# A fused attention and expert kernel: attention rows stored as float32, half pairs made for the first eight tiles only

## The chip, the cores and the metric

The kernel runs on one core of one Trainium2 chip. The metric is the device time of one execution in microseconds: the median of three runs is 897.36 us, from 895.99 to 898.08. The core's engines run side by side, each with a queue of its own: TensorE (PE in the profile, its weight loads PEld), VectorE (DVE), ScalarE (ACT), GpSimd (POOL) and SyncE (SP), which here only issues DMAs. ScalarE and GpSimd issue DMAs too.

## The reference

Three steps follow each other on 2304 tokens of 512 values. The first is an attention through 32 memory slots a head, for 4 batches and 8 heads:

```python
a = softmax(phi, axis=2)                       # over the 32 slots
k_m = einsum('bhsm,bhsd->bhmd', a, k); v_m = einsum('bhsm,bhsd->bhmd', a, v)
x = softmax(q @ k_m.T / 8) @ v_m               # as rows of 512 values, one a token
logits = x @ w_gate + log1p(exp(x @ w_noise)) * noise
out[mask] += weight * (relu(x[mask] @ w1[e]) @ w2[e])     # the two best of 8 experts
h = out @ w_in; result = (h * cos(h)) @ w_out
```

The second routes each token to its two best experts of 8 (512 to 1024 to 512), the third is a dense block (512 to 2048 to 512). All is float32; the kernel makes its products from pairs of halves: a float16 high part, and a float16 low part that is the float32 value less the high part.

## The kernel before

**Attention.** The 2304 tokens are 18 tiles of 128 rows. `k_gen` (L629) makes the 32 keys and values of a batch, `t_gen` (L728) one tile: scores, softmax, transposes, then the product `x` in PSUM. ScalarE copies `x` to `xs`, 128 x 512 in float32 (L769), and 32 gate columns to the routing's buffer (L775). Then the rows are split: ScalarE copies `xs` to float16 (L780), GpSimd subtracts that from `xs` for the low half (L782), and SP stores both, `hl`, as one row of 1024 float16 values in the DRAM tensor `xd` (L783). For the last two tiles this step is held back behind the routing's logarithm and the first gathers (L779, L781, L838 to L840). `xs` and `hl` take their slots from the pool `lp`, which has seven of 2 KB a partition (L77); later the experts' outputs, a zero tile and a scratch tile of ScalarE's share it.

**Routing.** `route` (L413) runs twice on VectorE, for tiles 0 to 7 and for tiles 8 to 17. Each run ends with a table of indices: `idxA` (L510), from tiles 0 to 7 alone, two columns of 128 slots for each expert (the first group); and `idxB` (L513), three columns for each expert, the last one 96 wide (the second group, 352 slots), of any tile. The one-hot rows for the table are made at L496 and L501.

**Experts.** `gather_x` (L906) has GpSimd gather 128 rows of `xd` into a tile `xg` (three buffers) by an indirect DMA, and SP turn it with a transposing DMA into `xT`, halves and all. `turn_x` (L920) is the turn by itself, for the groups that are gathered long ahead. `l1` (L924) multiplies a group by w1 in TensorE, `l1_out` (L942) makes the halves of the result on ScalarE and VectorE; `l2` (L950) multiplies 128 rows by w2. The weights come as float32 and are split by ScalarE (`w_hi`) and VectorE (`w_lo`). The first expert is special: its first group starts once `idxA` is there, while the second routing runs; `l2_first` (L972) then does its w2 products, high halves of w2 first and low halves behind, while the second group is gathered.

**Order.** What the engines run in which order is written out by hand: `at(t, f, ...)` (L86) plans a call at a time, with a lead that sets its priority, and `issue` sorts the calls. `gated(key)` and `chain(key, ...)` (L282, L286) put an instruction behind a named one on its own engine. The change moves calls between L835 and L856 and between L1262 and L1318. `tA` (L841) is the planned time of the step between the two routings, and `x` in L1292 to L1318 the running time of the experts. `overflow` (L1001) is a loop for experts with more than 608 rows.

Of the kernel before, what the change touches and what calls it, by code (L numbers as in the profile page):

```python
# [21 lines left out]
P = 128  # L22
# [43 lines left out]
def fused_kernel(ctx, tc, phiT, qT, kv, wgn, noise, w1, w2, wi, wo, out):  # L66
    nc = tc.nc
    V, A, G, T, SP = nc.vector, nc.scalar, nc.gpsimd, nc.tensor, nc.sync

    xd = nc.dram_tensor("xd", (N, 2 * DM), F16).ap()  # L70
    yd = nc.dram_tensor("yd", (YROWS, DM), F32).ap()
    wst = nc.dram_tensor("wst", (2 * NCH, P, 2048), F16).ap()

# [97 lines left out]
    def l2k(shape, dt, name):  # L171
        return lp.tile(shape, dt, tag="l", name=name)
# [555 lines left out]
    def t_gen(t):  # L728

        sc = scb[:, t % 2]  # L730
        for p0, n, b in segs(t):
            c0 = (t % 8) * P + p0
            for c in range(4):
                T.matmul(sc[p0:p0 + n, 64 * c:64 * c + 64], lhsT=qt[t // 8][:, c, c0:c0 + n],  # L734
                         rhs=bdkt[b][:, c, :], start=True, stop=True)
        yield
        sv = sc.rearrange("p (h m) -> p h m", m=M)
        mx = ap.tile([P, H], F32, tag="smx", name="smx")
        V.tensor_reduce(mx, sv, axis=AX.X, op=OP.max)
        dk = sds[t % 4]  # L740
        dv = dk[:, :, 0:M]
        V.tensor_tensor(dv, sv, mx[:, :, None].to_broadcast([P, H, M]), op=OP.subtract)
        yield
        A.activation(dv, dv, AF.Exp, scale=0.125)
        yield
        su = ap.tile([P, H], F32, tag="ssm", name="ssm")
        V.tensor_reduce(su, dk, axis=AX.X, op=OP.add)
        last[f"t{t}V"] = V.reciprocal(su, su)
        d = ap.tile([P, 2 * P], F32, tag="d", name="d")
        G.tensor_tensor(d.rearrange("p (h m) -> p h m", m=M), dv, su[:, :, None].to_broadcast([P, H, M]), op=OP.mult)  # L750
        yield
        pt = ptb[:, t % 2]
        for g in range(2):
            last[f"t{t}T"] = T.transpose(pt[:, g * P:(g + 1) * P], d[:, g * P:(g + 1) * P], ident)
        eT = ap.tile([P, 2, P], F32, tag="e2T", name="e2T")
        last[f"t{t}E"] = A.activation(eT.rearrange("p g s -> p (g s)"), pt, AF.Copy)
        yield
        ahead = t + 1 if t in AHEAD else None
        x = aps.tile([P, 2, 512], F32, tag="x", name="x")
        with gated(f"t{ahead}T" if ahead else f"tab0_{NA - 1}" if t == NT - 1 else None):  # L760
            for p0, n, b in segs(t):
                pn = slice(p0, p0 + n)
                for g in range(2):
                    last[f"t{t}P"] = T.matmul(x[pn, g, 0:272], lhsT=eT[:, g, pn], rhs=bdv[b][:, g, :], start=True,  # L764
                                              stop=True)
        yield
        xs = l2k([P, DM], F32, "xs")
        with gated(f"t{ahead}E"):
            A.activation(xs.rearrange("p (g d) -> p g d", g=2), x[:, :, 0:256], AF.Copy,  # L769
                                          scale=sT[:, 0, t:t + 1] if len(segs(t)) > 1 else sbs[segs(t)[0][2]][:, 0:1])  # L770
        g = ROUTE_OF[t]
        if t == GROUPS[g][0]:
            n = GROUPS[g][1] - GROUPS[g][0]
            lgb[g] = rg(g, "lgb", n, 2, 2 * E)
        last[f"t{t}A"] = A.activation(lgb[g][:, t - GROUPS[g][0]], x[:, :, 256:272], AF.Copy)  # L775
        yield
        hl = l2k([P, 2 * DM], F16, "hl")
        hv = hl.rearrange("p (w d) -> p w d", w=2)
        with gated({NT - 2: f"t{NT - 1}A", NT - 1: "ln"}.get(t)):  # L779
            A.activation(hv[:, 0], xs, AF.Copy)  # L780
        with gated("gather" if t >= NT - 2 else None):  # L781
            G.tensor_tensor(hv[:, 1], xs, hv[:, 0], op=OP.subtract)  # L782
        SP.dma_start(xd[t * P:(t + 1) * P, :], hl)  # L783
        yield

    def load_small():
# [48 lines left out]
    a_end = a_of(NT - 1) + 9.5  # L835
    for i in range(NT):
        g = t_gen(i)
        stages(g, [a_of(i) + x for x in t_steps[:-1 if i >= NT - 2 else None]])  # L838
        if i >= NT - 2:
            at(a_end - 0.4499 + 0.0001 * (i - NT + 2), next, g, None, lead=a_end - 0.45 - a_of(i) - t_steps[-1])  # L840
    R1, tA, LA = a_end - 0.5, a_end - 0.45, 60.0  # L841
    r0 = route(0)
    for t, n in ((12, 7), (13, 7), (14, 6)):
# [3 lines left out]
    for c in range(4):  # L847
        at(a_of(7 + c) + 8.0, e0, w_square, 0, c)
        at(a_of(12 + c) + 8.0, e0, w_hi, 0, c)
        at(a_of(17) + 7.3 + 0.01 * c if c < 2 else tA + 0.0001 * c, e0, w_lo, 0, c)  # L850
        if c:
            at(tA + 0.0003 + 0.0001 * c, e0, w_square, 1, c, lead=tA - a_of(17) - 8.0)
        else:
            at(a_of(17) + 8.0, e0, w_square, 1, c)
        at(tA + (0.0017, 0.0018, 0.0025, 0.0035)[c], e0, w_hi, 1, c)
        at(tA + 0.0096 + 0.00001 * c, e0, w_lo, 1, c)  # L856
    at(a_of(11) + 7.0, e0_scale, 0)
    at(tA + 0.0015, e0_scale, 1)

# [46 lines left out]
    def gather_x(e, part, turn=True):  # L906
        c0, c1 = parts[part]
        idx = idxA if part == 0 else idxB
        xT[e, part] = xp.tile([P, 8, (c1 - c0) * P], F16, tag=f"x{part}", name=f"x{part}")
        for c in range(c0, c1):  # L910
            g = xg[e, c] = xp.tile([P, 2 * DM], F16, tag="xg", name="xg", bufs=3)
            col = e * (c1 - c0) + c - c0
            last["gather"] = G.indirect_dma_start(out=g, out_offset=None, in_=xd[0:NA * P] if part == 0 else xd,  # L913
                                 in_offset=bass.IndirectOffsetOnAxis(ap=idx[:, col:col + 1], axis=0))
            if turn:
                tr = SP.dma_start_transpose(out=xT[e, part][:, :, (c - c0) * P:(c - c0 + 1) * P], in_=g)
        if e == 0:
            last["load"] = tr

    def turn_x(e, part, c):  # L920
        c0 = parts[part][0]
# [79 lines left out]
    def overflow():  # L1001
# [4 lines left out]
        with tc.For_i(0, n, 1, iteration_sync="staggered") as u:  # L1006
# [4 lines left out]
            for t in range(NT):  # L1011
                for k in range(2):
# [7 lines left out]
            io = small.tile([P, 1], I32, tag="io", name="io")  # L1020
            V.tensor_scalar(io, tb[:, 0:1], float(TB), None, op0=OP.add)
            g = l2k([P, 2 * DM], F16, "og")
            G.indirect_dma_start(out=g, out_offset=None, in_=xd,
                                 in_offset=bass.IndirectOffsetOnAxis(ap=io[:, :1], axis=0))
            xh = l2k([P, 8, P], F16, "oxh")
            SP.dma_start_transpose(out=xh, in_=g)
            x = l2k([P, 4, P], F32, "ox")
            V.tensor_tensor(x, xh[:, 0:4], xh[:, 4:8], op=OP.add)
            wa, wb = [], []
# [232 lines left out]
    X = [a_end + 0.5]  # L1262
    at(tA + 0.0094, next_pools)
    at(tA, gather_x, 0, 0, lead=LA)
    for f in range(8):
        at(tA + 0.002 + 0.001 * f, l1, 0, 0, f, lead=LA)
        at(tA + 0.002 + 0.001 * f, l1_out, 0, 0, f, lead=LA)
# [22 lines left out]
        return x  # L1290

    x = X[0]  # L1292
    at(x - 0.05, gather_x, 0, 1)
    at(x - 0.04, gather_x, 1, 0)
    for e in range(E):
        if e:
# [12 lines left out]
        if e == E - 1:  # L1309
            break  # L1310
        if e == 0:
            at(x + 0.1, gather_x, 1, 1)
        elif e < E - 1:
            at(x + 0.1, gather_x, e + 1, 1, False)
            for c in range(CA, NST):
                at(x + 4.0 + 0.5 * (c - CA), turn_x, e + 1, 1, c)
        for c in range(CA if e == 0 else 0, NST):
            x = put_l2(x, e, c)  # L1318

# [190 lines left out]
```

## Time and profile before

| what | before |
|---|---|
| median of three runs | 897.36 us |
| the profiled execution, its own time | 897.48 us |
| its span, first to last instruction | 895.5 us |
| PE busy | 861.0 us (96%) |
| DVE busy | 584.1 us (65%) |
| ACT busy | 465.0 us (52%) |
| POOL busy | 214.7 us (24%) |
| DMA packets | 146.66 MB, mean 164 GB/s |

The profile is that of one execution. An engine's busy time is the union of its instructions; times in the views are counted from the start of the span. "Releaser" is who ended a wait. A chain of waits goes back from the last instruction, at each step to what released it, or to the instruction before it on its engine. Attention and routing take up the first 104 us, the first expert's products run between 104 and 160 us with the second routing beside them, the others up to 515 us, the dense block from there.

### The profile page before, as it was taken

Reading aid. Unit: us, or ns where it says so; the run is one execution under the profiler, and the core shown is the slowest. Engines: PE = TensorE matmul, PEld = TensorE weight load, DVE = VectorE, ACT = ScalarE, POOL = GpSimd, SP = SyncE. Lnnn points to the kernel's source line nnn. Section 1 sums busy time; section 2 is a strip of 40 time slices with the busy share of each in tenths; the row PEclk is TensorE's granted clock in tenths of the full one; section 3 lists DMA queues with packets and bytes.
Section 4 is the critical chain, followed back from the end, with each engine's and each line's share of the span. In section 5 each row is a group of like instructions: output and inputs, shape, how many; then the busy total and the mean of one; then the engine's idle time right before and its main releaser. Section 6 shows DMA issues by size and latency. Waiting matters only on the chain.

```text
span 895.5 us, 16091 instructions
## 1 busy us (share of the span) xinstructions
PE 861.0 (96%) x6328; PEld 523.5 (58%) x6328; DVE 584.1 (65%) x1248; ACT 465.0 (52%) x830; POOL 214.7 (24%) x242
## 2 busy tenths in 40 slices
PE   5997599999999999999999999999999999999997
PEld 3875355757566574757566576654444444444564
DVE  3559853775668576866752389999877654465564
ACT  3588526566677677667762345453434322322233
POOL 1355321110111102010101154443532222222221
PEclk9898599999999999999999999999999999999999
DMA  9982459879989879796963623331522001100001
GB/s 350 395 329 83 129 159 224 293 221 314 221 298 272 275 237 309 251 322 252 258 253 133 196 71 83 71 94 48 119 58 61 25 0 24 48 1 1 1 24 47
DMA packets 109629, 146.66 MB, mean 164 GB/s; under 512 B 65776, under 2 KB 68720, under 8 KB 107504
## 3 DMA queue, kind: packets, MB, share of 16 engines
q1 hardware_dynamic: 89840, 103.95, 37.9%
q0 software_dynamic: 6080, 19.93, 7.7%
q10 hardware_dynamic: 13632, 21.74, 6.7%
q8 instruction: 50, 0.82, 0.4%
q14 instruction: 27, 0.22, 0.1%
HBM read 95.26 MB, written 35.13 MB: 146 GB/s over the span
## 4 chain that ended last, share of the span: by engine, by line
PE 85%; DVE 7%; ACT 4%; issue 2%; DMA 1%; ACTq 1%; SPq 0%; POOL 0%; DVEq 0%
PE y L289 22%; PE h L289 20%; PE g L289 19%; PE o L289 18%; PE kp L664 1%; DVE tt L289 1%; DMA kvt<-in_kv 1%; PE sc L734 1%; DVE ty L289 1%; PE x L764 1%; ACT junk L289 1%; ACT tt L289 1%; DVE ohp L501 1%; PE sums L289 1%; ACTq L289 1%
## 5 line engine op out<-in xcount | busy, mean ns | idle before, releaser
L289 PE MATMUL h<-x,w 128*128 128x352 f16 (+1 forms) x1536 | 205.2, 295 | 0.8 <-DVE hT L289 0.6
L289 PE MATMUL y<-w,hT 128*128 128x512 f16 (+2 forms) x1920 | 203.2, 294 | 1.1 <-issue 0.5
L289 PE MATMUL g<-x2T,win 128*128 128x256 f16 (+1 forms) x1152 | 202.2, 326 | 0.0
L289 PE MATMUL o<-wout,gT 128*128 128x512 f16 x864 | 201.5, 379 | 0.0
L289 PEld LDWEIGHTS <-w 128*128 128x128 f16 x1536 | 151.2, 99 | 49.6 <-issue 1.0
L289 PEld LDWEIGHTS <-win 128*128 128x128 f16 x1152 | 112.6, 98 | 83.7
L289 PEld LDWEIGHTS <-hT 128*128 128x128 f16 (+2 forms) x1920 | 106.3, 100 | 92.3 <-issue 3.6
L289 POOL TENSOR_TENSOR gT<-ty,gT 128x256 f16<-128x256 f32 (+1 forms) x96 | 90.8, 946 | 245.1 <-ACT gT L289 244.9
L289 ACT ACTIVATE tt<-tt,hp 128x256 f32<-128x256 f32 (+1 forms) x96 | 59.0, 615 | 158.4 <-DVE tt L289 151.9
L289 PEld LDWEIGHTS <-gT 128*128 128x128 f16 x864 | 84.5, 98 | 91.9
L289 DVE SCALAR_TENSOR_TENSOR hT<-h,hT 128x352 f16<-128x352 f32 (+1 forms) x128 | 59.4, 470 | 70.6 <-ACT hT L289 65.0
L289 DVE SCALAR_TENSOR_TENSOR ty<-g,wis,bct 128x256 f32<-128x256 f32 (+1 forms) x96 | 58.8, 613 | 63.8 <-PE g L289 62.4
L289 DVE SCALAR_TENSOR_TENSOR w<-raw,wsc,w 128x1024 f16<-128x1024 f32 x64 | 80.9, 1278 | 18.1 <-ACT w L289 15.9
L289 DVE SCALAR_TENSOR_TENSOR ty<-g,fac,tt 128x256 f32<-128x256 f32 (+1 forms) x96 | 59.0, 615 | 45.3 <-ACT tt L289 44.5
L289 ACT ACTIVATE hT<-h 128x352 f16<-128x352 f32 (+1 forms) x128 | 53.5, 421 | 64.4 <-PE h L289 51.1
L289 ACT ACTIVATE gT<-ty 128x256 f16<-128x256 f32 (+1 forms) x96 | 50.2, 523 | 61.3 <-DVE ty L289 57.3
L913 POOL DMA_INDIRECT xg<-xd,idxB x24 | 26.4, 1100 | 209.2 <-DMA x<-xg 196.3
L289 ACT ACTIVATE w<-raw,wsc 128x1024 f16<-128x1024 f32 x64 | 72.0, 1142 | 3.8 <-ACT o L289 3.8
L289 DVE SCALAR_TENSOR_TENSOR tt<-tt,ty 128x256 f32<-128x256 f32 (+1 forms) x96 | 69.6, 725 | 3.0
L289 ACT ACTIVATE junk<-raw 128x1024 bf16<-128x1024 f32 x64 | 67.3, 1052 | 3.8 <-ACT o L289 3.3
L289 ACT ACTIVATE o<-y,ysc 128x512 f32<-128x512 f32 (+1 forms) x40 | 26.6, 665 | 63.1 <-PE y L289 60.4
L289 POOL DMA_INDIRECT y<-yd,sidx x36 | 35.9, 998 | 82.5 <-DMA yd<-o 75.6
(230 smaller groups left out, 714.9 us busy)
## 6 DMA issues: line engine op xcount, KB each, us to landing
raw<-in_w SPq DMA_DIRECT2D x32, 1024.0 KB
kvt<-in_kv SPq DMA_DIRECT2D x9, 1024.0 KB
yd<-o ACTq DMA_DIRECT2D x32, 256.0 KB
cvt<-in_wi SPq DMA_DIRECT2D x8, 1024.0 KB
wst<-cvt SPq DMA_DIRECT2D x16, 512.0 KB
cvt<-in_wo SPq DMA_DIRECT2D x8, 1024.0 KB
yd<-zero ACTq DMA_DIRECT2D x14, 512.0 KB
xd<-hl SPq DMA_DIRECT2D x18, 256.0 KB
```

What stands on the lines that cost most here:

```text
L289: last[key] = fn(*a, **kw)
L501: o = V.tensor_scalar(ohp[:, k], iota_r, pf[:, t + q, k:k + 1], tokb[:, t + q:t + q + 1], op0=OP.is_equal, op1=OP.mult)
L664: T.matmul(kp[32 * j:32 * j + 32, g, :], lhsT=es[i][:, 32 * h:32 * h + 32], rhs=kvv[:, :, h * D:(h + 1) * D], start=(i == 0), stop=(i == 4))
L734: T.matmul(sc[p0:p0 + n, 64 * c:64 * c + 64], lhsT=qt[t // 8][:, c, c0:c0 + n], rhs=bdkt[b][:, c, :], start=True, stop=True)
L764: last[f"t{t}P"] = T.matmul(x[pn, g, 0:272], lhsT=eT[:, g, pn], rhs=bdv[b][:, g, :], start=True, stop=True)
L913: last["gather"] = G.indirect_dma_start(out=g, out_offset=None, in_=xd[0:NA * P] if part == 0 else xd, in_offset=bass.IndirectOffsetOnAxis ...
```

## The change

The DRAM tensor `xd` shrinks to the first eight tiles, and a tensor `xf` with float32 rows of all 18 tiles is added; a row has 2 KB in either. Every tile stores `xs` to `xf`; tiles 0 to 7 also make and store `hl`. First groups are gathered from `xd` as before. Second groups are gathered from `xf`, and their halves are made behind the gather, in a tile `xh` of the pool `lp`: for the first expert by ScalarE and VectorE (`split_0`), for the others by GpSimd, which copies and subtracts (`split_x`), in the overflow loop by ScalarE and VectorE. The hold on the last two tiles' halves goes. The first expert's second gathers, splits and turns are planned just behind the high-half products of `l2_first`, and the fourth quarter of the first expert's `w_lo` for w2 behind the splits. The other experts' turns of second groups are planned 8.0 us behind the gathers' call, where it was 4.0; expert 1's, which stood with their gathers, are planned in the same way.

```diff
-    xd = nc.dram_tensor("xd", (N, 2 * DM), F16).ap()
+    xd = nc.dram_tensor("xd", (NA * P, 2 * DM), F16).ap()
+    xf = nc.dram_tensor("xf", (N, DM), F32).ap()
...
-        hl = l2k([P, 2 * DM], F16, "hl")
-        hv = hl.rearrange("p (w d) -> p w d", w=2)
-        with gated({NT - 2: f"t{NT - 1}A", NT - 1: "ln"}.get(t)):
+        SP.dma_start(xf[t * P:(t + 1) * P, :], xs)
+        if t < NA:
+            hl = l2k([P, 2 * DM], F16, "hl")
+            hv = hl.rearrange("p (w d) -> p w d", w=2)
             A.activation(hv[:, 0], xs, AF.Copy)
-        with gated("gather" if t >= NT - 2 else None):
             G.tensor_tensor(hv[:, 1], xs, hv[:, 0], op=OP.subtract)
-        SP.dma_start(xd[t * P:(t + 1) * P, :], hl)
+            SP.dma_start(xd[t * P:(t + 1) * P, :], hl)
...
-        stages(g, [a_of(i) + x for x in t_steps[:-1 if i >= NT - 2 else None]])
...
+        stages(g, [a_of(i) + x for x in t_steps])
...
-        at(tA + 0.0096 + 0.00001 * c, e0, w_lo, 1, c)
+        at(tA + (0.0096 if c < 3 else 0.01285) + 0.00001 * c, e0, w_lo, 1, c)
...
-            last["gather"] = G.indirect_dma_start(out=g, out_offset=None, in_=xd[0:NA * P] if part == 0 else xd,
+            G.indirect_dma_start(out=g if part == 0 else g.bitcast(F32), out_offset=None, in_=xf if part else xd,
                                  in_offset=bass.IndirectOffsetOnAxis(ap=idx[:, col:col + 1], axis=0))
+            if part and e:
+                x = g.bitcast(F32)
+                xg[e, c] = l2k([P, 2 * DM], F16, "xh")
+                split_x(xg[e, c], x)
...
+    def split_0(c):
+        x = xg[0, c].bitcast(F32)
+        xg[0, c] = l2k([P, 2 * DM], F16, "xh")
+        hv = xg[0, c].rearrange("p (w d) -> p w d", w=2)
+        chain("A", A.activation, hv[:, 0], x, AF.Copy)
+        chain("V", V.tensor_tensor, hv[:, 1], x, hv[:, 0], op=OP.subtract)
+        turn_0(0, 1, c)
+
+    def split_x(hl, x, fast=False):
+
+        hv = hl.rearrange("p (w d) -> p w d", w=2)
+        if fast:
+            A.activation(hv[:, 0], x, AF.Copy)
+            V.tensor_tensor(hv[:, 1], x, hv[:, 0], op=OP.subtract)
+        else:
+            G.tensor_copy(hv[:, 0], x)
+            G.tensor_tensor(hv[:, 1], x, hv[:, 0], op=OP.subtract)
...
+    at(tA + 0.0127, gather_x, 0, 1, False, lead=49.0)
+    for c in range(CA, NST):
+        at(tA + 0.01275 + 0.00001 * c, split_0, c, lead=49.0)
...
-    at(x - 0.05, gather_x, 0, 1)
...
         if e == 0:
-            at(x + 0.1, gather_x, 1, 1)
+            at(x + 0.1, gather_x, 1, 1, False)
+            for c in range(CA, NST):
+                at(x + 8.0 + 0.5 * (c - CA), turn_x, 1, 1, c)
         elif e < E - 1:
             at(x + 0.1, gather_x, e + 1, 1, False)
             for c in range(CA, NST):
-                at(x + 4.0 + 0.5 * (c - CA), turn_x, e + 1, 1, c)
+                at(x + 8.0 + 0.5 * (c - CA), turn_x, e + 1, 1, c)
```

## Rows read from the trace of the kernel before

**Rows 1.** busy us by stage: length, PE, PEld, DVE, ACT, POOL, clock, DMA share

```profile
48.00:60.00 12.00, 11.90 (x156) 9.61 (x155) 6.68 (x21) 9.21 (x29) 8.36 (x12) 1.00 1.03 377
60.00:74.00 14.00, 12.21 (x110) 10.17 (x108) 9.72 (x29) 13.87 (x40) 7.67 (x12) 1.00 0.39 148
74.00:93.00 19.00, 13.43 (x61) 8.85 (x62) 18.11 (x62) 13.82 (x29) 8.79 (x10) 0.71 0.23 85
104.00:120.00 16.00, 15.15 (x122) 12.03 (x121) 11.64 (x56) 7.20 (x13) 1.21 (x3) 0.84 0.22 76
160.00:480.00 320.00, 319.65 (x2772) 210.20 (x2770) 215.41 (x404) 218.71 (x347) 32.12 (x27) 1.00 0.83 260
```

**Rows 2.** the chain of waits from 55 to 190: start us, length us, what

```profile
73.92 1.05 DVE rc L430
...
93.09 0.16 DVE idxA L510
```

**Rows 3.** VectorE's timeline: start, us, line, operation, out<-in, shapes, count

```profile
73.92 1.05 DVE L430 TENSOR_TENSOR rc<-rc,rw 128x64 f32<-128x64 f32 x1
...
76.68 0.24 DVE L435 TENSOR_TENSOR ry<-rl,rlgp 128x64 f32<-128x64 f32 x1
...
79.11 0.85 DVE L448 TENSOR_TENSOR oh<-rc,rk 128x64 f32<-128x64 f32 x1
...
82.03 1.17 DVE L453 TENSOR_TENSOR m<-oh,oh 128x64 f16<-128x64 f32 x1
...
85.49 1.68 DVE L496 TENSOR_TENSOR oha<-acode,af 128x240 f16<-128x240 f16 x2
87.10 3.75 DVE L501 TENSOR_SCALAR ohp<-iota_r,pf,tokb 128x128 f16<-128x128 f16 x12
90.77 0.31 DVE L496 TENSOR_TENSOR oha<-acode,af 128x160 f16<-128x160 f16 x1
91.01 0.97 DVE L501 TENSOR_SCALAR ohp<-iota_r,pf,tokb 128x128 f16<-128x128 f16 x4
...
120.31 4.86 DVE L289 SCALAR_TENSOR_TENSOR w<-raw,wsc,w 128x1024 f16<-128x1024 f32 x4
```

**Rows 4.** GpSimd's timeline, the same columns

```profile
81.97 1.15 POOL L782 TENSOR_TENSOR hl<-xs,hl 128x512 f16<-128x512 f32 x1
...
121.22 1.18 POOL L913 DMA_INDIRECT xg<-xd,idxB  x1 [0.30 <-issue]
```

**Rows 5.** SP's queue, three of its DMA issues

```profile
41.70 1.21 SPq L783 DMA_DIRECT2D xd<-hl  x1
...
100.53 1.23 SPq L916 DMA_TRANSPOSE x<-xg  x1
...
125.37 1.23 SPq L916 DMA_TRANSPOSE x<-xg  x1
```

**Rows 6.** TensorE's timeline, products of the first expert

```profile
103.83 2.72 PE L289 MATMUL h<-x,w 128*128 128x256 f16 x12
...
119.36 10.52 PE L289 MATMUL y<-w,hT 128*128 128x512 f16 x48
129.72 10.90 PE L289 MATMUL h<-x,w 128*128 128x352 f16 x72
```

**Rows 7.** groups by line and shape: busy us, mean ns, idle before and releasers

```profile
L782 POOL TENSOR_TENSOR hl<-xs,hl 128x512 f16<-128x512 f32 x18 | 21.0, 1168 | 8.5 <-ACT hl L780 6.3 <-issue 1.8 <-PE pt L754 0.2
...
L289 DVE SCALAR_TENSOR_TENSOR chl<-y,cmx,chl 128x512 f16<-128x512 f32 x18 | 13.2, 745 | 0.7 <-ACT chl L289 0.7
...
L780 ACT ACTIVATE hl<-xs 128x512 f16<-128x512 f32 x18 | 11.4, 632 | 0.0
```

**Rows 8.** DMA packets that start from 44 to 46 us

```profile
DMA packets 402, 0.78 MB, mean 388 GB/s; under 512 B 19, under 2 KB 268, under 8 KB 402
```

**Rows 9.** ScalarE's timeline, tile 4's float32 row tile

```profile
49.76 0.69 ACT L769 ACTIVATE xs<-x,sT 128x512 f32<-128x512 f32 x1
```

More of the change, by code (lines that the diff above doesn't have):

```diff
@@ L837, in fused_kernel @@
         g = t_gen(i)
-        stages(g, [a_of(i) + x for x in t_steps[:-1 if i >= NT - 2 else None]])
-        if i >= NT - 2:
-            at(a_end - 0.4499 + 0.0001 * (i - NT + 2), next, g, None, lead=a_end - 0.45 - a_of(i) - t_steps[-1])
+        stages(g, [a_of(i) + x for x in t_steps])
     R1, tA, LA = a_end - 0.5, a_end - 0.45, 60.0
@@ L912, in gather_x, with turn_0 @@
             col = e * (c1 - c0) + c - c0
-            last["gather"] = G.indirect_dma_start(out=g, out_offset=None, in_=xd[0:NA * P] if part == 0 else xd,
+            G.indirect_dma_start(out=g if part == 0 else g.bitcast(F32), out_offset=None, in_=xf if part else xd,
                                  in_offset=bass.IndirectOffsetOnAxis(ap=idx[:, col:col + 1], axis=0))
+            if part and e:
+                x = g.bitcast(F32)
+                xg[e, c] = l2k([P, 2 * DM], F16, "xh")
+                split_x(xg[e, c], x)
             if turn:
-                tr = SP.dma_start_transpose(out=xT[e, part][:, :, (c - c0) * P:(c - c0 + 1) * P], in_=g)
+                turn_0(e, part, c)
+    def turn_0(e, part, c):
+        o = slice((c - parts[part][0]) * P, (c - parts[part][0] + 1) * P)
+        tr = SP.dma_start_transpose(out=xT[e, part][:, :, o], in_=xg[e, c])
         if e == 0:
             last["load"] = tr
+    def split_0(c):
[13 more added lines that the diff above has]
+            G.tensor_tensor(hv[:, 1], x, hv[:, 0], op=OP.subtract)
     def turn_x(e, part, c):
@@ L1022, in overflow @@
             g = l2k([P, 2 * DM], F16, "og")
-            G.indirect_dma_start(out=g, out_offset=None, in_=xd,
+            G.indirect_dma_start(out=g.bitcast(F32), out_offset=None, in_=xf,
                                  in_offset=bass.IndirectOffsetOnAxis(ap=io[:, :1], axis=0))
+            gs = l2k([P, 2 * DM], F16, "ogs")
+            split_x(gs, g.bitcast(F32), True)
             xh = l2k([P, 8, P], F16, "oxh")
-            SP.dma_start_transpose(out=xh, in_=g)
+            SP.dma_start_transpose(out=xh, in_=gs)
             x = l2k([P, 4, P], F32, "ox")
```

## The prediction

> **What bounds the kernel now.** I read the busy time by stage first. From 160 to 480 us TensorE works 319.65 of 320 us, VectorE 215.41 [rows 1]: the experts are bound by TensorE's own work, which the change leaves alone. So what can move is the front. From 48 to 60 us TensorE is full (11.90 of 12) and the DMA engines too (share 1.03); from 60 to 74 ScalarE is full (13.87 of 14); from 74 to 93 VectorE is (18.11 of 19) [rows 1]. The chain of waits agrees: it enters VectorE at 73.92 us and ends there with the first table of indices at 93.09 [rows 2].
>
> Next I read what VectorE does in that stretch. The reader should compare equal instructions. A 64-wide TENSOR_TENSOR takes 0.24 us at 76.68, but 1.05 at 73.92 and 1.17 at 82.03; twelve one-hot rows take 3.75 us at 87.10, 0.31 each, but four at 91.01 take 0.97, 0.24 each [rows 3]. GpSimd tells why: its subtract for the low half of a tile runs from 81.97 for 1.15 us, to 83.12, and the VectorE instruction of 82.03 ends just behind, at 83.20 [rows 3, 4]. These instructions, with both sides in SBUF, stand still while GpSimd's subtract runs. There are six such holds between 73.9 and 93.
>
> **Part 1: no halves for tiles 8 to 17 (L777 to L783).** Gone are ten ScalarE copies of 0.632 us and ten GpSimd subtracts of 1.168 us [rows 7]. The six holds lie under the subtracts of tiles 10 to 15; those of 16 and 17 are queued behind the first gathers. What the six give back: 1.05 - 0.24 and 1.17 - 0.24, 0.8 and 0.9 us; for the twelve one-hot rows 3.75 - 12 x 0.24 = 0.9; for the pair of 240-wide comparisons 1.68 - 2 x 0.4 = 0.9, with 0.4 scaled up from 0.31 for a 160-wide one; the comparison at 79.11 took 0.85, 0.6 more than the clean row, and one more hold is like it [rows 3]. Sum 4.7, and all of it on the chain, since VectorE has under 1 us idle in that stage. I take **-4.7 us** for the time of the first indices. The bounds are 0 (another engine steps in) and -4.7.
>
> Before 74 ScalarE loses three copies, 3 x 0.63 = 1.9 us [rows 7], but TensorE is busy 12.21 of those 14 us [rows 1], so 1.8 is the most.
>
> Behind the first indices the path is gather, turn, first product. The second turn is issued at 100.53 and the products begin at 103.83, 3.3 us later [rows 5, 6]; nothing in gather or turn of this group changes, so it moves with the indices. Two more holds on VectorE and tile 17's copy go away behind 93 too, but TensorE works 15.15 of the 16 us from 104 on [rows 1], so at most 0.85 comes of them. I take 0, since TensorE's order there is kept.
>
> **Part 2: float32 stores (new line behind L776).** All 18 tiles are now stored from xs as well, 256 KB each as a half pair is: 26 stores for 18, 2.1 MB more. Until 46 us the DMA engines still bring q (the packets under 2 KB, 388 GB/s), and three weight loads of 1 MB are issued before the first store at 41.70 [rows 5, 8]: 3.1 MB at 0.39 MB/us is 8 us, so the first store lands near 54. That was harmless, because xs came free with GpSimd's subtract. Now xs is held until its store has landed, and the pool of seven slots (L77) is full with xs and hl of tiles 0 to 2 and xs of tile 3. Tile 4's xs, which ran at 49.76 [rows 9], would find a slot near 54 to 55: 5 us late at worst. Against that, the work of tiles 4 to 7 can slip while TensorE makes the keys of the last batch; tiles 8 and on take one slot each; and ScalarE gains up to 1.8 by 74. I set the two against each other and take **0**; the bounds are -1.8 and +5. Later stores find free DMA engines (share 0.39 from 60, 0.23 from 74 [rows 1]), and nobody waits for them before the second indices.
>
> **Part 3: the first expert's second group.** Gathers move the same 2 KB a row, so 1.18 us on GpSimd stays [rows 4]. Their issue moves ahead in the written order, but they wait for idxB as before. Behind each comes a copy on ScalarE (0.632), a subtract on VectorE (0.745 by the nearest row), and only then the turn [rows 7]. The last turn is issued at 125.37 [rows 5] and the 352-wide products start at 129.72, without a wait behind the first sums that began at 119.36 [rows 6]. With 0.2 for two handovers the last turn's issue comes to 125.37 + 0.63 + 0.75 + 0.2 = 126.95; SP issues three at 1.23 each, closer together now, so say 127.3. With the 3.3 us from issue to use the products start at 130.6, 0.9 late. VectorE's last low part of w2 now stands behind the three subtracts: 4.86 / 4 = 1.2 us [rows 3], done near 128.2, and TensorE asks for it at 119.36 + 38/48 x 10.52 = 127.7. That delay lies inside the other. I take **+1.0**, bounds 0 (the landing of the turn was ahead of need) and +2.5 (all of it in a row).
>
> **Part 4: 21 more tiles of the second groups, experts 1 to 7.** Each adds a copy and a subtract on GpSimd, 2 x 1.17 at most, 49 us in 320, where it is busy 32 [rows 1]. Turns are planned 4 us later, and on SP the loads behind them wait for the splits. The three split tiles also hold slots that the experts' outputs use. The cover is TensorE's work, a whole group ahead; I take **0**, bounds 0 and +8. If the cover failed, one microsecond late on each of seven groups would be +7. The overflow loop's split runs in no iteration of this profile.
>
> **Sum.** -4.7 + 0 + 1.0 + 0 = -3.7 us. The profiled execution took 897.48 us (span 895.5, 1.98 around it), 0.12 above the median of 897.36. So 897.48 - 3.7 = 893.8, and 893.7 against the median; I say **893.7**. No change that a measurement can tell is within 0.2%, 1.8 us, thus 895.6 to 899.2.
>
> **Rivals.**
> First, slots and stores stall the attention: the 5 us of part 2 are not made up. For it: DMA share 1.03 and TensorE full from 48 to 60 [rows 1]. Against: the keys of the last batch fill TensorE meanwhile. 893.7 + 5 = 898.7, no change to tell or a little slower.
>
> Second, VectorE is not alone as bound: with the holds gone TensorE (13.43 of 19) or ScalarE (13.82 of 19) [rows 1] or the plain latency between them sets the time of the first indices, and only some 2 us come. -2 + 1 gives 896.4, no change to tell. Against it: both have over 5 us idle there.
>
> Third, the other side: GpSimd's splits hold VectorE among the experts. Place: 160 to 480 us; the holds of rows 3, at up to 1.17 us, now hit the weight splits, 42 instructions. VectorE has 104 us idle there, so it decides only where the products' four banks run out behind a held VectorE, that is where two holds meet in one group. If 21 splits cost TensorE 0.4 us each, +8.4: 902. It wins from 4.7 us of lost TensorE time on, since then the front's gain is spent. The Trainium skill ("SBUF — State Buffer", section "SBUF: two separate sides") has a rule that speaks for this rival: GpSimd and a VectorE instruction with two SBUF inputs compete for one pair of ports, which whoever starts first keeps for the whole instruction. By that rule the weight splits, with two SBUF inputs, would be held as the comparisons are; the trace agrees for the front (1.17 against 0.24 us) and shows no such pair among the experts.
>
> That the change doesn't do what it says fits here as well: GpSimd's work isn't saved but moved, 10 subtracts gone and 42 instructions come.
>
> **How the numbers follow.** Forecast (the holds go, 891 to 895.6): 0.58. First rival 0.15, two thirds of it within 0.2%. Second 0.15, within. Third 0.12, slower. Faster 0.58, same 0.25, slower 0.17. The low end takes the gains of part 1 and of ScalarE whole and nothing for part 3: 897.4 - 4.7 - 1.8 = 890.9. The high end takes in the first rival, 898.7; beyond it lies mainly the third. The forecast's own range is 890.9 to 895.6.
>
> **What would show it.** Right: the 64-wide comparisons between 74 and 93 us take 0.24 us, idxA comes near 88.5, the products start near 99, TensorE shows a gap of about 1 us ahead of the first 352-wide product, and 160 to 480 shifted stays full. Wrong: ScalarE waits for a landing between 46 and 56; the first indices stay near 93 with VectorE idle ahead of them; or TensorE waits for hT among the experts.

## The result, and the profile after

The changed kernel takes 905.24 us (median of four runs, 904.30 to 905.44) where the kernel before takes 897.45 beside it: ratio 1.0092, 95% interval 1.0079 to 1.0105. It is 7.8 us slower, outside the range and on the other side of the forecast. The profiled execution has a span of 903.1 us against 895.5, so 7.6 us are to be found in the traces. Lines of the kernel from L289 on have moved by one or more: L290 is what L289 was.

Busy time by stage of the changed kernel; the columns are those of [rows 1], and the stage from 120 to 130 us is new:

```profile
48.00:60.00 12.00, 10.98 (x160) 9.10 (x161) 7.30 (x26) 6.93 (x21) 3.98 (x7) 1.00 1.05 402
...
74.00:93.00 19.00, 13.45 (x69) 8.05 (x69) 14.54 (x59) 15.57 (x36) 4.46 (x6) 1.00 0.33 122
...
120.00:130.00 10.00, 6.66 (x31) 2.92 (x30) 3.89 (x6) 1.97 (x3) 3.64 (x3) 1.00 0.78 174
160.00:480.00 320.00, 316.18 (x2827) 208.25 (x2813) 224.30 (x400) 217.78 (x345) 75.10 (x60) 0.99 0.80 259
```

Three stages differ from before. From 48 to 60 us ScalarE does 6.93 us of work instead of 9.21; from 120 to 130 TensorE has 3.3 us idle; from 160 to 480 it lacks 3.5 us that it did not lack before. VectorE, on the other hand, is at 14.54 of 19 from 74 to 93: the holds are gone.

**The front.** ScalarE's copies of the rows of tiles 3 and 4, VectorE's one-hot rows and the first indices (timelines of the two engines):

```profile
44.38 0.69 ACT L770 ACTIVATE xs<-x,sb 128x512 f32<-128x512 f32 x1
...
56.93 0.69 ACT L770 ACTIVATE xs<-x,sT 128x512 f32<-128x512 f32 x1
...
82.55 2.63 DVE L502 TENSOR_SCALAR ohp<-iota_r,pf,tokb 128x128 f16<-128x128 f16 x10
87.97 0.54 DVE L502 TENSOR_SCALAR ohp<-iota_r,pf,tokb 128x128 f16<-128x128 f16 x2 [2.79 <-PE tab L506]
...
90.74 0.17 DVE L511 TENSOR_SCALAR idxA<-tab 128x16 int32<-128x16 f32 x1
```

The one-hot rows take 0.26 us each, not 0.31 as under a hold [rows 3]. But tile 4's rows come at 56.93 instead of 49.76 [rows 9], and that in an execution that had tile 3's rows early, at 44.38, where the kernel before had them at 45.63 (its timeline of ScalarE). Between the two tiles lie 12.5 us instead of 4.1. In the trace these rows wait for the store of tile 1's rows, which lands at 55.78. The late tiles' products then stand among the table's on TensorE, VectorE waits 2.79 us for the table, and the first indices come at 90.74 instead of 93.09 [rows 2]. Counted from tile 2's rows (42.08 before, 40.83 here), that is 49.91 us instead of 51.01: 1.1 us gained of 4.7. The other 1.25 are this execution's early start.

**The first expert's second group.** VectorE, SP, GpSimd and TensorE of the changed kernel (timelines), and one piece of its chain of waits:

```profile
117.10 3.67 DVE L290 SCALAR_TENSOR_TENSOR w<-raw,wsc,w 128x1024 f16<-128x1024 f32 x3
120.68 1.89 DVE L290 TENSOR_TENSOR xh<-xg,xh 128x512 f16<-128x512 f32 x3
...
121.39 4.64 SPq L923 DMA_TRANSPOSE x<-xh  x3
...
121.64 1.75 POOL L912 DMA_INDIRECT xg<-xd,idxA  x1 [4.31 <-DVE xh L290]
...
124.09 6.32 DMA x<-xh
...
116.14 10.52 PE L290 MATMUL y<-w,hT 128*128 128x512 f16 x48
130.45 12.58 PE L290 MATMUL h<-x,w 128*128 128x352 f16 x72 [3.78 <-DMA x<-xh]
```

The y products begin at 116.14, 3.2 us earlier than in [rows 6]; the 352-wide ones at 130.45, 0.7 us later. Three low parts of w2 stand ahead of the subtracts on VectorE, so the first turn is issued only at 121.39. The third, issued at 124.09, lands 6.32 us later; the second expert's gathers, which begin at 121.64 because the first subtract gave a buffer back, run beside it, and its own turns are queued behind it. TensorE is idle for 3.78 us, and then the 72 products take 12.58 us instead of 10.90.

**The sixth expert** (some expectations below call it the fifth). SP, ScalarE's queue (ACTq) and TensorE of the kernel before (timelines; these rows were not read for the prediction):

```profile
336.85 5.64 SPq L289 DMA_TRANSPOSE x<-xg  x3
345.11 0.34 SPq L289 DMA_DIRECT2D wst<-cvt  x1
...
345.99 2.70 SPq L289 DMA_DIRECT2D raw<-in_w  x2
...
364.16 2.00 ACTq L289 DMA_DIRECT2D yd<-zero  x1
...
361.92 8.03 PE L289 MATMUL h<-x,w 128*128 128x256 f16 x72
370.30 0.38 PE L289 MATMUL sums<-wmx,ones 128*128 128x2 f32 x2 [0.35 <-ACT junk L289]
```

The same place in the changed kernel, and the pieces of the chain of waits there:

```profile
347.99 0.34 SPq L290 DMA_DIRECT2D wst<-cvt  x1
348.77 5.86 SPq L290 DMA_TRANSPOSE x<-xh  x3
...
355.30 0.95 SPq L290 DMA_DIRECT2D raw<-in_w  x2
...
369.50 2.90 PE L290 MATMUL h<-x,w 128*128 128x256 f16 x25 [0.89 <-issue]
372.84 1.47 PE L290 MATMUL h<-x,w 128*128 128x256 f16 x12 [0.44 <-DVE hT L290]
376.04 0.38 PE L290 MATMUL sums<-wmx,ones 128*128 128x2 f32 x2 [1.73 <-ACT junk L290]
...
355.83 13.99 DMA raw<-in_w
...
369.84 2.06 ACTq L290
...
371.95 0.38 ACT hT L290
```

All work here lies 2.7 us later than before. The store `wst`, which waits for VectorE, is where it was (345.11 + 2.7 = 347.8), but the three turns now stand behind it instead of ahead of it. They need 5.86 us of SP, and the two weight loads behind them are issued at 355.30 where 345.99 + 2.7 = 348.7 was due: 6.6 us late. The second lands at 369.82. At 369.84 ScalarE's queue issues a DMA, the store of a zero tile, which takes 2.06 us, and only then comes the next copy hT, for which TensorE waits. The kernel before has the same store at the same place, issued at 364.16, and there TensorE is idle for 0.35 us only.

The account of the 7.6 us, from the starts of these rows: early start -1.25, front -1.1 (together the -2.4 of the first products); y products another -0.9; the 352-wide products 4.0 late and 1.7 slower; the sixth expert 5.0 (3.0 idle, 1.7 slower products behind it, 0.3 on the way there); the rest 0.2.

### The profile page after: what moved, and what is told of

The parts are those of the page before. It is cut to its first block, busy times and chain, and to the rows that moved or that the text cites. A ratio compares the mean times of both kernels' runs of the same rounds, so it can differ in the third digit from the quotient of the medians.

```text
span 903.1 us, 16156 instructions
## 1 busy us (share of the span) xinstructions
PE 860.9 (95%) x6328; PEld 521.1 (58%) x6328; DVE 588.8 (65%) x1251; ACT 462.9 (51%) x823; POOL 254.8 (28%) x274
## 4 chain that ended last, share of the span: by engine, by line
PE 76%; DVE 4%; issue 4%; DMA 3%; ACT 3%; POOL 1%; ACTq 0%; DVEq 0%; POOLq 0%; SPq 0%
PE y L290 19%; PE g L290 19%; PE h L290 19%; PE o L290 18%; DMA raw<-in_w 2%; DVE tt L290 1%; DVE ty L290 1%; ACT tt L290 1%; DMA x<-xh 1%; POOL xg L912 1%; PE sums L290 1%; ACT o L290 1%; ACTq L290 0%; DMA yd<-o 0%; DMA xg<-xf,idxB 0%
## 5 line engine op out<-in xcount | busy, mean ns | idle before, releaser
L290 PE MATMUL h<-x,w 128*128 128x352 f16 (+1 forms) x1536 | 208.0, 297 | 7.9 <-DMA x<-xh 3.8
L290 PE MATMUL y<-w,hT 128*128 128x512 f16 (+2 forms) x1920 | 203.2, 294 | 0.6 <-ACT hT L290 0.3
L290 PE MATMUL g<-x2T,win 128*128 128x256 f16 (+1 forms) x1152 | 202.2, 326 | 0.0
L290 PE MATMUL o<-wout,gT 128*128 128x512 f16 x864 | 201.5, 379 | 0.0
L290 PEld LDWEIGHTS <-w 128*128 128x128 f16 x1536 | 151.9, 100 | 59.0 <-issue 7.9
L290 PEld LDWEIGHTS <-win 128*128 128x128 f16 x1152 | 112.6, 98 | 83.7
L290 POOL TENSOR_TENSOR gT<-ty,gT 128x256 f16<-128x256 f32 (+1 forms) x96 | 90.8, 946 | 245.7 <-ACT gT L290 245.5
L290 PEld LDWEIGHTS <-hT 128*128 128x128 f16 (+2 forms) x1920 | 106.2, 100 | 91.8 <-issue 3.0
L290 ACT ACTIVATE tt<-tt,hp 128x256 f32<-128x256 f32 (+1 forms) x96 | 59.0, 615 | 158.5 <-DVE tt L290 152.2
L290 PEld LDWEIGHTS <-gT 128*128 128x128 f16 x864 | 84.5, 98 | 91.9
L290 DVE SCALAR_TENSOR_TENSOR hT<-h,hT 128x352 f16<-128x352 f32 (+1 forms) x128 | 59.2, 469 | 75.1 <-ACT hT L290 70.0
L290 DVE SCALAR_TENSOR_TENSOR ty<-g,wis,bct 128x256 f32<-128x256 f32 (+1 forms) x96 | 58.8, 613 | 64.3 <-PE g L290 64.1
L290 DVE SCALAR_TENSOR_TENSOR w<-raw,wsc,w 128x1024 f16<-128x1024 f32 x64 | 83.1, 1311 | 17.8 <-ACT w L290 17.6
L290 ACT ACTIVATE hT<-h 128x352 f16<-128x352 f32 (+1 forms) x128 | 53.6, 421 | 75.9 <-PE h L290 60.7
L290 DVE SCALAR_TENSOR_TENSOR ty<-g,fac,tt 128x256 f32<-128x256 f32 (+1 forms) x96 | 59.0, 615 | 45.1 <-ACT tt L290 44.3
L290 ACT ACTIVATE gT<-ty 128x256 f16<-128x256 f32 (+1 forms) x96 | 50.2, 523 | 61.3 <-DVE ty L290 57.3
L290 ACT ACTIVATE w<-raw,wsc 128x1024 f16<-128x1024 f32 x64 | 72.0, 1141 | 5.6 <-ACT o L290 3.8
L290 DVE SCALAR_TENSOR_TENSOR tt<-tt,ty 128x256 f32<-128x256 f32 (+1 forms) x96 | 69.6, 725 | 3.0
L290 ACT ACTIVATE junk<-raw 128x1024 bf16<-128x1024 f32 x64 | 67.3, 1052 | 3.9 <-ACT o L290 3.4
L290 POOL DMA_INDIRECT y<-yd,sidx x36 | 36.0, 999 | 89.6 <-DMA yd<-o 79.3
L290 ACT ACTIVATE o<-y,ysc 128x512 f32<-128x512 f32 (+1 forms) x40 | 26.6, 665 | 57.8 <-PE y L290 44.7
L942 POOL CAST xh<-xg 128x512 f16<-128x512 f32 x21 | 15.9, 756 | 132.4 <-DMA xg<-xf,idxB 42.3
```

The source lines that it names most:

```text
L290: last[key] = fn(*a, **kw)
L942: G.tensor_copy(hv[:, 0], x)
```

## The experiments

Twelve runs were made. For each I give the ratio to the kernel before on the same chip, and read the profiled execution, which is one of four to ten, by three marks. The "front" runs from ScalarE's copy of tile 2's rows to the first indices. Within it lies a scan on VectorE (L466 before, L467 after), the first instruction behind TensorE's rank products of the routing; the first four holds of the prediction come ahead of it, the last two behind. Starts from the timelines of ScalarE and VectorE, and the lengths between them, in us:

| kernel | tile 2's rows | scan | first indices | to the scan | from there on | front |
|---|---|---|---|---|---|---|
| before | 42.08 | 83.71 | 93.09 | 41.63 | 9.38 | 51.01 |
| changed | 40.83 | 80.12 | 90.74 | 39.29 | 10.62 | 49.91 |
| changed, again (`c4_after_again`) | 42.14 | 82.61 | 93.25 | 40.47 | 10.64 | 51.11 |
| `a4_hlroom` | 41.93 | 81.10 | 88.53 | 39.17 | 7.43 | 46.60 |
| `b3_all` | 42.59 | 81.77 | 89.20 | 39.18 | 7.43 | 46.61 |
| `c1_all_subs` | 40.09 | 79.38 | 89.41 | 39.29 | 10.03 | 49.32 |
| `c2_all_halves` | 41.70 | 83.57 | 93.65 | 41.87 | 10.08 | 51.95 |

The "experts' stretch" runs from the first 256-wide product (103.83 in [rows 6]) to the last expert's group of 25 y products: 400.98 before, 410.73 changed. The gap is the one before the 352-wide products. The start of the front moves by up to 3 us from one execution to the next, so the marks tell more than one time does.

**Turns back in their old place** (`a1_turn4`)

```diff
-                at(x + 8.0 + 0.5 * (c - CA), turn_x, e + 1, 1, c)   # e >= 1
+                at(x + 4.0 + 0.5 * (c - CA), turn_x, e + 1, 1, c)
```

> The change with one number undone: the turns of second groups, experts 2 to 7, are placed 4 us behind the end of the first products again, not 8. Theory (order on SP): in the changed kernel the three turns at 348.8 stand behind a store that waited for VectorE and ahead of two weight loads, which issue at 355.3 instead of 348.7; TensorE then loses about 3.0 us in idle time and 1.7 us at the lower granted clock between 364 and 395. With the turns in their old place this is gone: 4.7 us less than the changed kernel, about 900.5 us. Rival (the splits on GpSimd slow VectorE or the transfers, wherever the turns stand): within 1 us of 905.2. A third outcome is a wait of SP for a split that is not done, which would make it slower than 905.2.

903.04 us, ratio 1.0092 (1.0057 to 1.0128). That is neither outcome in the expectation, and the interval is too wide to tell by itself; the changed kernel on the same chip took 907.53 (the last run below). SP and TensorE around the sixth expert (timelines) tell more:

```profile
339.77 5.59 SPq L290 DMA_TRANSPOSE x<-xh  x3
348.40 0.35 SPq L290 DMA_DIRECT2D wst<-cvt  x1
...
349.85 1.80 SPq L290 DMA_DIRECT2D raw<-in_w  x2
...
364.79 8.03 PE L290 MATMUL h<-x,w 128*128 128x256 f16 x72
373.94 0.38 PE L290 MATMUL sums<-wmx,ones 128*128 128x2 f32 x2 [1.11 <-ACT junk L290]
```

The turns hide in the wait ahead of the store again, the loads are issued 1.5 us behind it instead of 7.3, and the idle time goes from 3.1 to 1.1 us. The stretch is 404.64 us, and of the 3.7 us still above the kernel before 3.4 are the gap of the first expert. No split was late: the last turn leaves SP at 345.36, 3.0 us ahead of the store.

**No splits among the experts** (`a3_nosplit`)

```diff
-                                 in_=xf if part else xd, ...     # then split_x on GpSimd
+            if part and e:
+                idx, col = idxA, e * CA + (c - c0) % CA          # rows of halves, turned as they lie
+                                 in_=xd if half else xf, ...     # half = part == 0 or e > 0
```

> The change without the splits of experts 1 to 7: their second groups gather rows of halves by the first group's indices and are turned as they lie, so the output rows of these groups are not the reference's. 21 casts and 21 subtracts on GpSimd are left out; the turns stay 8 us behind the end of the first products. Theory (the place of the turns on SP costs 4.7 us, the splits nothing): within 1 us of the changed kernel's 905.2. Rival (the splits cost, through VectorE or through GpSimd's queue): 4 to 6 us less, 899 to 901.

905.84 us, ratio 1.0097 (1.0068 to 1.0125), as the theory said. Without one split, the loss of the sixth expert is all there; SP and TensorE:

```profile
350.56 6.16 SPq L290 DMA_TRANSPOSE x<-xg  x3
...
357.39 0.95 SPq L290 DMA_DIRECT2D raw<-in_w  x2
...
375.52 1.47 PE L290 MATMUL h<-x,w 128*128 128x256 f16 x12 [2.42 <-DVE hT L290]
378.71 0.38 PE L290 MATMUL sums<-wmx,ones 128*128 128x2 f32 x2 [1.73 <-ACT junk L290]
```

So the place of the turns on SP made this loss, not the splits.

**The store of zeros later** (`d1_zerolate`, the last one run)

```diff
     for u in range(0, MAXOV, 2):
-        at(X[1] + 10.0 * u, clear, u)
+        at(X[1] + 10.0 * u + (8.0 if u == 20 else 0.0), clear, u)
```

> The changed kernel with one store of zeros moved 8 us back in ScalarE's order, from ahead of the sixth expert's second hT copy to behind the seventh; SP's order and all else stay. In the changed kernel that store is issued at 369.84, 0.02 us behind the landing of a late weight load (369.82) with which it shares nothing but one of the eight completion counters that the issues take in turn, and it takes 2.06 us; the hT copies behind it wait. Theory A (the late load reaches TensorE through that store): the second hT copy runs near 368, and the idle time of 3.1 us near 364 to 376 falls to 1.5 us or less; the experts' stretch is 1.5 to 3.5 us shorter than 409.3 to 410.7. Theory B (the late load reaches TensorE through the split of its own weights, which stands between the hT copies): the first copies come earlier, but ScalarE then waits for the load until 369.8, and the idle time stays within 0.7 us of 3.1.

902.40 us, ratio 1.0078 (1.0044 to 1.0113). The five times lie between 898.30 and 907.82 and decide nothing; the trace is that of the fastest. ScalarE (timeline), and TensorE's products in the chain of waits:

```profile
366.41 0.38 ACT L290 ACTIVATE hT<-h 128x256 f16<-128x256 f32 x1 [0.26 <-PE h L290]
...
373.13 0.39 ACTq L290 DMA_DIRECT2D yd<-zero  x1
...
363.65 7.99 PE h L290 x72
```

The loads are as late as in the changed kernel (issued from 354.10, the second landed at 368.04), and yet TensorE is not idle here: its 72 products take 7.99 us, all in a row. The stretch is 404.17 us, and the 3.2 us above the kernel before are the first expert's gap, 3.46. The late load harmed through one store; theory B is out. That it was the counter is shown by times, not by a change of the counter alone. In the trace of the changed kernel the store's instruction lists a wait for one completion counter, and the last DMA ahead of it that reports there is the second load. In all seven executions that have the late loads and the store in its old place the store starts 0.02 us behind that load's landing. With the turns in their old place the second load reports to another counter, but it is early as well. And the edit took the store's own 2 us away with its wait.

**VectorE's order in the first expert** (`a2_subfirst`)

```diff
-        at(tA + (0.0096 if c < 3 else 0.01285) + 0.00001 * c, e0, w_lo, 1, c)
+        at(tA + (0.01276, 0.012775, 0.0128, 0.01281)[c], e0, w_lo, 1, c)
```

> The change with VectorE's order in the first expert altered: the three subtracts of the split stand between the four low-half subtracts of w2 (one of those, then subtract, one, two subtracts, two), instead of behind three of them. Theory (VectorE's order made the turns late): the first turn issues near 119.0 instead of 121.4, the third near 122 instead of 124.1; the idle 3.8 us before the first 352-wide product goes to 0.5 or less, and the 72 products take 10.9 us again instead of 12.6: 3.5 to 5.5 us less, 900 to 902 us. Rival (the third turn is late because the second expert's gathers run beside it, 6.3 us to landing instead of 3.1): the gathers come earlier too, the third turn still lands 5 to 6 us after its issue, and 2 us or more of the gap stay: 903 to 904.

907.18 us, ratio 1.0138 (1.0098 to 1.0178): no gain. SP:

```profile
118.78 3.03 SPq L923 DMA_TRANSPOSE x<-xh  x2
123.87 1.23 SPq L923 DMA_TRANSPOSE x<-xg  x1
125.19 1.29 SPq L923 DMA_TRANSPOSE x<-xh  x1
```

The first turn is 2.6 us earlier, as expected. But the second expert's gathers come earlier too, and its first turn, which waits for one of them, got ahead of the third turn in the queue, which lands 4.25 us after its issue: 3.1 us of gap stay. The rival was right in its outcome, by a nearer reason than it gave.

**Holding the second expert's gathers** (`b1_hold`), then with the new order as well (`b2_subhold`)

```diff
+        if (e, part) == (1, 0):
+            last["held"] = G.tensor_copy(sT[:, 0, 0:1], xT[0, 1][:, 0, 2 * P:2 * P + 1])
...
+            with gated("held"):
                 G.indirect_dma_start(...)
```

> The change with one wait added: the gathers for the second expert are held on GpSimd until the third turn of the first expert's second group has landed (GpSimd reads one column of it first). VectorE's order stays. Theory A (the third turn is slow because those gathers run beside it): it issues near 124 as before but lands 3.1 us later, near 127.3, instead of 6.3 us; the gap before the first 352-wide product goes from 3.8 to about 0.8 us, and the lower clock behind it goes too: 2.5 to 5 us less than the changed kernel's 905.2, beside the same front. Theory B (VectorE's order alone made the gap): the third turn still lands near 130 and the time stays.

900.39 us, ratio 1.0042 (1.0026 to 1.0059). SP, GpSimd and TensorE:

```profile
123.11 3.98 SPq L926 DMA_TRANSPOSE x<-xh  x3
...
129.73 0.96 POOL L915 DMA_INDIRECT xg<-xd,idxA  x1 [0.51 <-issue]
...
129.02 10.90 PE L290 MATMUL h<-x,w 128*128 128x352 f16 x72 [0.65 <-DMA x<-xh]
```

VectorE's order is the changed kernel's, the turns are issued with the same lag, and yet the gap is 0.65 us: the third turn, issued at 125.81, lands at 128.98, in 3.2 us. The collision with the gathers was the larger part. (The hold keeps the second expert's own turns away as well; the two are not told apart.)

> The hold of the second expert's gathers and the new order on VectorE together (the subtracts between the low halves of w2). The run with the new order alone had the second expert's first turn ahead of the third turn on SP, and 3.1 us of gap; the hold puts that turn behind. Expected by both theories together: turns issue near 119, 120.5 and 122, the last lands near 125.2, ahead of the end of the y products near 126.6; gap 0 to 0.3 us. 5.5 us less than the changed kernel, about 899.7 us, of which the late weight loads of the fifth expert (4.7 us) are still there. If a gap over 1 us stays, something else holds the turns.

900.40 us, ratio 1.0045 (1.0030 to 1.0059). The turns land by 126.74, the y products end later, and the gap is gone. What this gives over holding alone, 0.65 us of gap, is under what the times can tell.

**Halves of the first tiles outside the slots** (`a4_hlroom`)

```diff
-            hl = l2k([P, 2 * DM], F16, "hl")
+            if t % 4 == 0:
+                hls.append(hs("hT", 0, [P, 4, 2 * DM], F16))
+            hl = hls[-1][:, t % 4]
```

> The change with the halves of the first eight tiles put into two buffers that lie unused until the first hT (four tiles of halves in each), so that the seven 2 KB slots hold the float32 rows alone. Theory (the slots, held until the stores landed, kept tile 4's rows back from 49.8 to 56.9): tile 4's rows come at about 50, ScalarE's work between 48 and 60 us goes from 6.9 back to about 9 us, and the first indices come at 88.5 to 89.5 instead of 90.7; 1 to 2.3 us less, 903 to 904. Rival (the chain of ScalarE and TensorE over the last tiles sets the first indices whatever the slots do): first indices at 90.7, within 0.7 us of 905.2.

903.40 us, ratio 1.0069 (1.0050 to 1.0089). ScalarE's copies of the rows of tiles 3 and 4 and, ahead of them, of three halves; the first indices on VectorE:

```profile
44.44 1.66 ACT L786 ACTIVATE hT<-xs 128x512 f16<-128x512 f32 x3
...
46.69 0.69 ACT L772 ACTIVATE xs<-x,sb 128x512 f32<-128x512 f32 x1
...
50.82 0.69 ACT L772 ACTIVATE xs<-x,sT 128x512 f32<-128x512 f32 x1
...
88.53 0.16 DVE L511 TENSOR_SCALAR idxA<-tab 128x16 int32<-128x16 f32 x1
```

The slots were the stall: tile 4 follows tile 3 by 4.1 us again, and the front is 46.60 us, 3.3 less than in the changed kernel. (Counted from tile 3's rows it would be 4.5, but 1.2 of that is not a gain: the copies of three halves now run ahead of those rows, which come 4.76 us behind tile 2's and not 3.55.) The 3.3 us lie behind the scan: VectorE no longer waits 2.79 us for the table. In the second execution of the changed kernel the front is 1.2 us longer, all of it ahead of the scan; why is not shown. The 1 to 2.3 us that I expected came from the time of the first indices alone and missed that execution's early start.

**All four mends in one** (`b3_all`)

> All four mends in one kernel: halves of the first tiles outside the slots, new order on VectorE, gathers of the second expert held, and the turns of experts 2 to 7 four us behind the first products. Theory (the change's three losses are separate and its gain is the 4.7 us of the front): first indices near 88.5, no gap before the 352-wide products, no idle time of TensorE among the experts: 905.2 - 2.2 - 5.5 - 4.7 = 892.8 us, 4.6 us below the kernel before (ratio 0.995). If the losses only cover each other (a load that comes early meets another), 895 to 899.

892.49 us, ratio 0.9954 (0.9937 to 0.9971): faster than both kernels, 0.5% faster than the kernel before, and 0.3 us from the number expected. First indices at 89.20, a front of 46.61 us, no gap, a stretch of 400.13 us. The losses were separate: by the marks the front is 3.3 us shorter than in the changed kernel and the stretch 10.6. That the time came so near is in part luck, since 2.2 were expected of the front and this execution's front starts 1.8 us later.

**Subtracts on GpSimd put back** (`c1_all_subs`), **and the copies on ScalarE too** (`c2_all_halves`). Both start from the kernel with all mends.

```diff
+        else:                                    # c1: tiles 8 to 17
+            G.tensor_tensor(hls[2][:, t % 4, DM:], xs, hls[1][:, 3, :DM], op=OP.subtract)
...
-        if t < NA:                               # c2: copy and subtract for all, stored for t < NA
+        if True:
```

> The kernel with all four mends, and ten subtracts on GpSimd more, one behind the rows of each of tiles 8 to 17, of the shape and types of those that the change removed; their results go to a spare buffer and nothing is stored. Theory (VectorE was held by these subtracts): the 64-wide comparisons next to them take 0.9 to 1.2 us again instead of 0.24, the first indices move from 89.2 to 92 to 94 us, and the time rises by 3 to 4.7 us to 895.5 to 897. Rival (the front's gain came from ScalarE's ten copies, or from the stores): first indices within 1 us of 89.2, time within 1 us of 892.5.

895.34 us, ratio 0.9991 (0.9979 to 1.0003), 2.9 us above the kernel with all mends (3.3 by the ratios; that one ran on another chip). The holds are back; VectorE's pair of comparisons, which took 0.72 us without GpSimd's subtract beside it (81.90 in the changed kernel), and the scan, first with all mends, then in this run:

```profile
81.77 0.29 DVE L467 TENSOR_TENSOR_SCAN rcum<-same,rank 128x64 f32<-128x64 f16 x1 [1.35 <-PE rank L464]
...
79.38 0.28 DVE L467 TENSOR_TENSOR_SCAN rcum<-same,rank 128x64 f32<-128x64 f16 x1 [0.50 <-PE rank L464]
...
81.89 1.68 DVE L497 TENSOR_TENSOR oha<-acode,af 128x240 f16<-128x240 f16 x2
```

The first indices (89.41) seem not to move, but this execution starts early. The front is 49.32 us, 2.7 more than with all mends, and 2.6 of that lie behind the scan. Ahead of it VectorE is held as well (one 64-wide TENSOR_TENSOR takes 1.07 us, another 0.92), yet the scan comes only 0.1 us later: VectorE then waits 0.50 us for the rank products, and with all mends 1.35.

> The kernel with all four mends, and both halves of tiles 8 to 17 made as in the kernel before (ten copies on ScalarE, ten subtracts on GpSimd), into a spare buffer, not stored. Theory (VectorE's holds are the whole of the front's gain, ScalarE's copies are worth nothing): the same as with the ten subtracts alone, within 1 us. Rival (ScalarE's copies count too): 1 to 2.5 us above the run with the subtracts alone.

897.84 us, ratio 1.0010 (0.9995 to 1.0025), another 2.5 us on the same chip (1.7 by the ratios). The front is 51.95 us, 2.6 more, and all of it lies ahead of the scan. The rival was right here: ScalarE's ten copies cost as much as the ten subtracts. (The subtracts now wait for the copies too, which this run does not part from the copies themselves.) The front is 0.9 us longer than in the kernel before, which makes the same halves with fewer stores and holds two tiles' halves back; what of that costs the 0.9 is not shown.

**No splits, with all mends** (`c3_all_nosplit`; the edit of `a3_nosplit`)

> The kernel with all four mends without the splits of experts 1 to 7; their second groups gather rows of halves by the first group's indices, so the output rows of these groups are not the reference's. Theory (42 GpSimd instructions hidden behind TensorE cost nothing): within 1 us of 892.5. Rival (they slow VectorE or hold up gathers, which the kernel with all mends still pays): 1.5 us or more below it.

892.21 us, ratio 0.9938 (0.9920 to 0.9956), 0.3 us below the kernel with all mends, or 1.4 by the ratios, whose intervals overlap. Stage 160 to 480, first with all mends, then without the splits (columns as in [rows 1]):

```profile
160.00:480.00 320.00, 319.40 (x2743) 207.40 (x2741) 225.30 (x397) 216.38 (x343) 74.17 (x62) 1.00 0.81 259
```

```profile
160.00:480.00 320.00, 319.28 (x2751) 207.95 (x2749) 214.06 (x398) 216.86 (x344) 31.91 (x27) 1.00 0.82 258
```

With the splits GpSimd works 42 us more and VectorE 11 us more for the same instructions: it is held there as well. TensorE loses nothing: 319.40 against 319.28 us. The run without splits is idle for 1.9 us once, from 154.9 on, ahead of this stage, so the two times alone would not settle it.

**The changed kernel again** (`c4_after_again`)

> The changed kernel once more, unaltered, beside the others on this chip. If its three losses are of its order and not of one execution, they show again: tile 4's rows 6 to 9 us behind 50, a gap of 3 to 5 us before the first 352-wide product, and 2 to 5 us of idle time near 365 to 376. Time 904 to 906, about 12.5 us above the kernel with all mends.

907.53 us, ratio 1.0124 (1.0105 to 1.0143), 1.5 us above the end of what was expected. Tile 4's rows come 12.5 us behind tile 3's, the gap is 3.27 us, the 72 products take 12.31, and TensorE is idle for 3.2 us near 375: the three losses come back. This time the clock does not fall behind the idle time of the sixth expert (108 products in 15.31 us, 16.98 in the first execution).

## Why the prediction was wrong

The prediction had 893.8 us for the profiled execution, which took 905.15. Of the 11.35 us between them parts 1 and 2 together make 3.6 (-4.7 forecast, -1.1 measured), part 3 makes 3.8, part 4 makes 5.0 and the rest 0.2, less 1.25 of an early start.

**Part 1** (-4.7 on the first indices) has nearly the right size and the wrong working. With the slots free the front falls from 51.01 to 46.61 us, by 4.4. The step that failed is "all of it on the chain, since VectorE has under 1 us idle". With the copies gone, the four holds ahead of the scan are worth 0.1 us: VectorE waits longer for the rank products without them. The two behind it were priced at 0.9 each, and the subtracts are worth 2.6 there. ScalarE's copies, for which part 1 took nothing, are worth 2.6 ahead of the scan. So a busy share of 18.11 of 19 did not make VectorE the bound of that whole stage, and that the sum came near 4.7 is luck.

**Part 2** (0, bounds -1.8 and +5) is the second step that failed. The slots filled where it said, the first stores landed near 55 us (54 was its estimate), and tile 4 came 8.4 us further behind tile 3 than before. "I set the two against each other" was wrong: ScalarE's gain came ahead of the scan (41.63 us before, 39.29 in the changed kernel), and the stall came behind it, where VectorE waited for the table: 3.3 us. The bound was right, the value taken in it was not.

**Part 3** (+1.0, bounds 0 and +2.5) is the third. The 352-wide products lost 4.0 us against the y products, and 1.7 more by the clock. "0.2 for two handovers" put each subtract right behind its copy; but the first half, copied at 117.30, waited for VectorE until 120.68, since only the last of the four low parts of w2 had been moved behind the subtracts. And "the 3.3 us from issue to use" was taken from a turn that no gather ran beside; here it was 6.3 us to the landing. The change gives the gather buffer back at the subtract and not at the turn, so the next expert's gathers moved from behind the turns into them. Holding the gathers gave nearly all of it back.

**Part 4** (0, bounds 0 and +8) is the fourth. The prediction saw that "turns are planned 4 us later, and on SP the loads behind them" wait, and named TensorE's cover as the whole price. The cover holds for the turns and even for the late loads themselves. What it does not hold for is a store on ScalarE that waits for the second load's completion counter, and the copies hT behind that store: 3.0 us of idle time, and 1.7 of the clock. A wait that no dependency between the tiles makes was not in any step.

**Rivals.** The first (slots and stores) came true, at 3.3 us of its 5. The second came true for the way to the scan: with the copies gone the holds were worth 0.1 us there, while the copies of ScalarE, an engine that it names, were worth 2.6. The third is shown in its mechanism and refuted in its price: VectorE is held 11 us among the experts, at no cost. The Trainium skill ("SBUF — State Buffer", section "SBUF: two separate sides") has VectorE instructions with two SBUF inputs and GpSimd's reads compete for one pair of ports; the traces agree (VectorE busy 225.30 against 214.06 us). The third rival's time, 902, was nearest to the 905.24 measured, but by luck: the loss has other reasons.

## What to carry to other kernels

Where a buffer is given back earlier, ask which transfer was waiting for it, and what it will run beside. Where a DMA is moved on a queue, price what is queued behind it, not the moved DMA: three turns that nobody waited for cost 4.7 us in this execution, through two loads behind them and a store on another engine that waited for the counter of one. And a stage in which one engine is 95% busy can still have a second bound: take one engine's work away in an experiment before its whole time is put on the path.

## What was not expected of the hardware

A store issued by ScalarE waited for a weight load issued by SP with which it shared only a completion counter (369.84 against 369.82, and the same 0.02 us in six other executions). The wait stands with the store's instruction, so it is the program's, not one that the chip adds. A transposing DMA of 256 KB took 3.1 to 3.2 us from issue to landing where no gather of the next expert ran beside it, and 5.8 to 7.5 beside its gathers and turns (six executions). And the price of a gap on TensorE is not its length. Granted clock (third column from the end; 1.00 is 2.4 GHz, 0.50 is 1.2) of the changed kernel behind its two idle stretches:

```profile
132.00:134.00 2.00, 2.00 (x9) 1.03 (x7) 0.53 (x1) 1.06 (x2) 0.00 (x0) 0.50 1.10 254
...
378.00:380.00 2.00, 2.00 (x11) 1.40 (x10) 1.44 (x3) 0.29 (x1) 0.00 (x0) 0.50 0.06 24
```

In this execution the clock falls after work has begun again (near 131.7, work from 130.45; near 377.5, work from 376.04), and that costs 1.7 us each time. In the second execution of the same kernel it is at 0.50 already when work begins (0.50 from 132.5 on, work from 132.99): behind a gap of 3.27 us the 72 products take 12.31. Behind gaps of 3.1 to 3.5 us four executions kept 1.00 and took 10.90 us. What decides near there stays open.
